# A hand-ordered retention and MLP kernel with another order of the same steps

## The chip, the cores and the metric

The kernel runs on one core of a Trainium2 chip. The metric is device time in microseconds; the median of three runs is given, and beside it one execution taken by the hardware profiler. The engines are TensorE (PE in the profile; PEld is its weight load), VectorE (DVE), ScalarE (ACT), GpSimd (POOL) and SyncE (SP), which here only issues DMAs.

## What is computed

A retention layer with 8 heads of 64, over 4 batches of 768 tokens, and behind it an MLP that mixes tokens by phase. All inputs and the output are float32.

```
state = gamma[h] * state + k[:, :, t] (outer) v[:, :, t]      # for each token t
y[:, :, t] = q[:, :, t] @ state / sqrt(64)
x = y with the heads side by side                            # [4, 768, 512]
theta = x @ w_theta
y2 = w_tok_r @ (x * cos(theta)) + w_tok_i @ (x * sin(theta)) # over tokens, each batch
u = x + y2
out = u + max(u @ w_ch, 0)
```

## The kernel before

The work is cut into small steps, each a function with a short name and a number. One string, ORDER, lists about 880 such steps by hand; the program calls them in that order, so each engine receives its instructions in the order in which the steps stand, and each DMA queue too. Engines wait for each other by semaphores. A step's last letter, where it has one, names the engine or queue that does it: v VectorE, a ScalarE, p GpSimd, s SyncE.

The retention is done in 24 units n. A unit is 256 tokens (two chunks of 128) of four heads of one batch; units 2i and 2i+1 are the two halves of the heads, and three pairs make a batch.

- Lk, Lq, Lv (line 157) load k, q and v of a unit, 256 KB each. Lth and Lch (line 174) load w_theta and w_ch, 1 MB each, into one buffer, and Lw.r.t (line 185) a block of 128 rows of a token matrix, 384 KB. All of these are issued on SP's queue.
- ck casts k to bf16 (lines 137 and 139), cq scales q by the decay (line 279), cv scales v (line 285).
- Tk and Tq transpose k and q on TensorE (line 293), four 128x128 matmuls each, and E copies the result from PSUM to kqT. Dk does all three for a unit by one DMA transpose (line 309).
- G.n is 48 matmuls of 64x64 tiles: scores A of unit n (line 323), outputs Y of unit n-1 (line 393), state products ST of unit n (line 351). m masks the scores on VectorE (line 332). SU adds up the state (lines 363 to 367), SB copies it to bf16 (two pieces a unit), and I multiplies q by the state (line 380).
- XA takes the finished x, transposed, out of PSUM on ScalarE (line 413).

The MLP is done by token blocks of 128 tokens, C for its first part and t for its second, 24 of each, six a batch.

- Tx and Ex transpose x back through PSUM (line 427), or Dx does it by DMA (line 434). Hh is theta, four matmuls of 512 columns (line 441). CN are cosine and sine on ScalarE (line 448, two a block). z multiplies them by x (line 455).
- cw casts a row block of a token matrix, Tw transposes it with six matmuls (line 472), and Ew copies it to its place in wT. cth and cch cast w_theta and w_ch in quarters.
- M.t.s is the part of token mixing for output block t that comes from input block s: two matmuls of 512 columns (line 488). It needs z of block s in the same batch and wT of row block t.
- u adds x (line 495); Tu and Eu (line 500), or Du by DMA (line 510), transpose u; O multiplies by w_ch, four matmuls (line 515); f is the last sum with the maximum (line 521); SO stores 256 KB (line 526).
- The last block, 23, is done in two halves of columns: Mh, uh, Tuh, Euh, Oh, fh, SOh (lines 529 to 576).

warm.N issues N matmuls on zeros (line 258) whose result nobody reads. const1 to const7 set up constants.

Buffers tie steps together: kf, qf and vf have nine buffers each, wtok four, wrow three, kqb five, kqT four, xT four, uT three, and all transposes through PSUM share two banks (tag "tr"). A step that writes a buffer waits until its last reader is done.

Of the kernel before, what the change touches and what calls it, by code (L numbers as in the profile page):

```python
# [32 lines left out]
I.4 CN.1.0 Tx.3 ck.6.a G.5 cq.6.v Tq.6 Lv.7.s Lk.8.s CN.1.1 Lq.8.s z.0.p SU.5 SB.5.1.p Tk.6
cw.1.0.p cv.6.p Lw.0.1.s m.5 Lv.8.s Ex.3.a XA.4.1 Hh.3 XA.4.0 ck.7.p Tx.2 cq.7.p Lk.9.s E.6.v
Lq.9.s Hh.2 Ex.2.v CN.3.0 ck.8.p SB.5.0.a z.1.v Lw.1.1.s Tw.1.0 Lv.9.s Ew.1.0.v CN.3.1 cq.8.p I.5
cv.7.p CN.2.0 z.3.v cv.8.p G.6 XA.5.1 Tk.7 XA.5.0 Hh.5 Lk.10.s Tq.7 Tk.8 CN.2.1 m.6 CN.5.1 Lq.10.s
CN.5.0 SU.6 Hh.4 E.7.v SB.6.1.a Tq.8 SB.6.0.a Tx.4 M.0.0 I.6 cw.0.1.a G.7 z.2.v E.8.v Ex.4.v Tx.5
SU.7 CN.4.1 Lw.0.2.s M.0.1 Ex.5.v ck.9.p CN.4.0 cq.9.p M.0.2 XA.6.0 Tw.0.1 SB.7.1.p XA.6.1
SB.7.0.a Lw.1.2.s m.7 z.4.v Tk.9 M.0.3 Tq.9 Ew.0.1.a cw.1.1.p I.7 Lv.10.s Lk.11.s G.8 XA.7.0
Lq.11.s z.5.v E.9.a cv.9.p Tw.1.1 M.0.4 Ew.1.1.v XA.7.1 Lw.0.3.s M.0.5 u.0 Lw.1.3.s SU.8 SB.8.0.v  # L40
Hh.6 ck.10.p cq.10.p cw.0.2.p m.8 Lw.0.4.s cw.1.2.p Tk.10 Lw.1.4.s M.1.0 Lv.11.s M.1.1 CN.6.0
cw.0.3.p M.1.2 M.1.3 Tq.10 SB.8.1.a I.8 M.1.4 Tw.0.2 M.1.5 E.10.v Lch.s cw.1.3.p Lk.12.s Lq.12.s
Ew.0.2.v Tw.1.2 CN.6.1 cv.11.p G.9 Ew.1.2.a ck.11.a Hh.7 u.1 M.2.0 ck.12.p XA.8.0 CN.7.0 CN.7.1
M.2.1 cq.11.v cq.12.p cv.10.v SU.9 Lv.12.s Lk.13.s Tk.11 XA.8.1 SB.9.1.v M.2.2 Tq.11 cv.12.p M.2.3
# [565 lines left out]
```

## Time and profile before

| | us |
|---|---|
| median of three runs | 169.86 |
| lowest and highest | 169.74, 170.08 |
| the profiled execution | 170.49 |
| its span, first to last instruction | 168.8 |
| TensorE, matmuls busy | 156.0 |
| VectorE busy | 123.8 |
| ScalarE busy | 79.2 |
| GpSimd busy | 78.5 |

HBM read is 25.69 MB and written 6.29 MB in the span. A matmul's row in the profile holds its latency (379 ns for 512 columns), though the next one starts sooner; how far apart they follow is read in the chain of waits, which lists pieces of consecutive work with their start, their length and their number. A timeline row gives start, length, engine, line, operation, the tile written and the tiles read, how many, and in brackets the idle time of the engine before it with what ended it. A row of windows gives, for a stretch of time, the busy time and number of instructions of each engine, then TensorE's granted clock as a share, the mean share of the DMA engines and GB/s. Of the slices in the page, each stands for a fortieth of the span.

### The profile page before, as it was taken

The numbers are of one execution on the slowest core, as the hardware profiler recorded it, in microseconds if no ns is written. First come the engines' busy times: TensorE is split into PE (matmuls) and PEld (weight loads), VectorE is DVE, ScalarE is ACT, GpSimd is POOL, SyncE is SP. The second block draws the span as 40 slices with busy tenths as digits, with TensorE's granted clock in tenths as the row PEclk, the third lists the DMA queues.
The fourth block names the chain that finished last, engine by engine and source line by source line (L and its number), as shares of the span: only waits on it lengthen the run. The fifth ranks groups of instructions, "written<-read, shape, count | busy, mean of one in ns | idle before, by whom it ended". The sixth has DMA issues, their size and how long they took to land.

```text
span 168.8 us, 4924 instructions
## 1 busy us (share of the span) xinstructions
PE 156.0 (92%) x2017; PEld 89.0 (53%) x2044; DVE 123.8 (73%) x200; ACT 79.2 (47%) x159; POOL 78.5 (47%) x99
## 2 busy tenths in 40 slices
PE   7988794989899989999999999999999999999991
PEld 2555463557566655555645565554555444444660
DVE  3497979699999897899669979689737443526552
ACT  6346385587657755666322593674323544000030
POOL 3778377998932634669203658023354560000000
PEclk9999999599999999999999999999999999999999
DMA  4999999999799999999999188899998736335555
GB/s 141 296 290 332 329 322 289 274 319 350 257 283 329 221 232 292 254 207 309 305 244 227 65 188 209 124 276 168 269 230 133 197 62 186 93 93 194 88 188 186
DMA packets 68582, 38.20 MB, mean 226 GB/s; under 512 B 25936, under 2 KB 63056, under 8 KB 68560
## 3 DMA queue, kind: packets, MB, share of 16 engines
q1 hardware_dynamic: 67408, 35.92, 88.8%
q10 hardware_dynamic: 1152, 1.97, 3.5%
q8 instruction: 16, 0.26, 0.6%
q14 instruction: 6, 0.05, 0.1%
HBM read 25.69 MB, written 6.29 MB: 189 GB/s over the span
## 4 chain that ended last, share of the span: by engine, by line
PE 65%; DVE 14%; SPq 11%; DMA 4%; issue 2%; ACT 1%; DVEq 0%; ACTq 0%
PE y_ps L488 31%; PE o_ps L515 11%; PE th_ps L441 9%; SPq L157 9%; DVE z L455 5%; DMA qf<-in_q_dram 4%; DVE at L332 3%; PE at_ps L323 3%; PE r_ps L393 2%; PE r_ps L380 2%; PE y_ps L538 2%; DVE kqb L279 1%; PE kq_ps L293 1%; PE w_ps L472 1%; SPq L185 1%
## 5 line engine op out<-in xcount | busy, mean ns | idle before, releaser
L488 PE MATMUL y_ps<-z,wtr 128*128 128x512 bf16 x135 | 51.2, 379 | 1.0 <-DVE z L455 0.5
L488 PE MATMUL y_ps<-z,wti 128*128 128x512 bf16 x129 | 48.9, 379 | 0.4 <-issue 0.3
L413 ACT CAST xT<-r_ps 128x256 bf16<-128x256 f32 x48 | 16.9, 372 | 30.7 <-PE r_ps L351 19.6
L279 POOL TENSOR_TENSOR kqb<-qf,qsc 128x512 bf16<-128x512 f32 x20 | 23.7, 1189 | 14.1 <-DMA qf<-in_q_dram 13.7
L332 DVE TENSOR_TENSOR at<-at_ps,mask 128x1024 bf16<-128x1024 f32 x24 | 29.1, 1213 | 1.1 <-PE at_ps L323 1.0
L521 DVE SCALAR_TENSOR_TENSOR ot<-o_ps,u 128x512 f32<-128x512 f32 x23 | 15.8, 689 | 14.9 <-PE o_ps L515 14.8
L441 PE MATMUL th_ps<-wth,xT 128*128 128x512 bf16 x89 | 25.0, 395 | 1.4 <-POOL wth L139 1.0
L285 POOL TENSOR_TENSOR vb<-vf,vsc 128x512 bf16<-128x512 f32 x17 | 18.9, 1114 | 10.0 <-DMA vf<-in_v_dram 9.9
L515 PE MATMUL o_ps<-wch,uT 128*128 128x512 bf16 x88 | 23.2, 379 | 0.4 <-DVE wch L139 0.2
L488 PEld LDWEIGHTS <-wti 128*128 128x128 bf16 x138 | 13.5, 98 | 13.4 <-issue 1.1
L448 ACT ACTIVATE cs<-th_ps,halfpi 128x512 bf16<-128x512 f32 x24 | 16.5, 688 | 8.2 <-PE th_ps L441 5.8
L488 PEld LDWEIGHTS <-wtr 128*128 128x128 bf16 x138 | 13.5, 98 | 13.0
L495 DVE TENSOR_TENSOR u<-y_ps,x_sb 128x512 bf16<-128x512 f32 x23 | 15.8, 686 | 5.8 <-PE y_ps L488 5.8
L448 ACT ACTIVATE cs<-th_ps,zerob 128x512 bf16<-128x512 f32 x24 | 16.2, 687 | 5.7 <-PE th_ps L441 5.3
L455 DVE TENSOR_TENSOR z<-cs,x_sb 128x1024 bf16<-128x1024 bf16 x18 | 16.6, 936 | 2.9 <-ACT cs L448 2.7
L455 POOL TENSOR_TENSOR z<-cs,x_sb 128x1024 bf16<-128x1024 bf16 x6 | 12.9, 2153 | 6.6 <-DMA x_sb<-xT 3.9
L139 POOL CAST kqb<-kf 128x512 bf16<-128x512 f32 x16 | 10.6, 666 | 8.3 <-DMA kf<-in_k_dram 6.1
L441 PEld LDWEIGHTS <-xT 128*128 128x128 bf16 x96 | 9.0, 100 | 10.3 <-issue 1.8
L515 PEld LDWEIGHTS <-uT 128*128 128x128 bf16 x92 | 8.7, 98 | 9.5 <-issue 0.3
L137 ACT COPY uT<-u_ps 128x512 bf16<-128x512 bf16 x6 | 3.5, 589 | 21.3 <-PE u_ps L500 21.3
L258 PE MATMUL y_ps<-zero 128*128 128x512 bf16 x36 | 12.0, 447 | 1.4 <-DVE zero L194 1.3
L293 PE MATMUL kq_ps<-ident,kqb 128*128 128x128 bf16 x112 | 9.8, 223 | 2.2 <-DVE kqb L279 2.2
(74 smaller groups left out, 209.3 us busy)
## 6 DMA issues: line engine op xcount, KB each, us to landing
kf<-in_k_dram SPq DMA_DIRECT2D x24, 256.0 KB, 5.4
qf<-in_q_dram SPq DMA_DIRECT2D x24, 256.0 KB, 5.1
vf<-in_v_dram SPq DMA_DIRECT2D x24, 256.0 KB, 5.4
out_dram<-ot SPq DMA_DIRECT2D x16, 256.0 KB, 3.3
wtok<-in_moe_w_tok_r_dram SPq DMA_DIRECT2D x6, 384.0 KB, 6.1
wtok<-in_moe_w_tok_i_dram SPq DMA_DIRECT2D x6, 384.0 KB, 5.9
out_dram<-ot ACTq DMA_DIRECT2D x7, 256.0 KB, 2.1
w<-in_moe_w_theta_dram SPq DMA_DIRECT2D x1, 1024.0 KB, 8.4
```

Of the source, the lines that this page charges most:

```text
L157: queues[e].dma_start(out=t.rearrange("p h a d -> p h (a d)"), in_=src[b, h * HU:(h + 1) * HU, i * 2 * P:(i + 1) * 2 * P, :].rearrange("h ...
L279: engines[e].tensor_mul(in_blocks(kqb_of(n)[:, 1]), by_token(raw["qf", n]), _bcast_last(K["qsc"][:, i, :, h * HU:(h + 1) * HU], D))
L285: engines[e].tensor_mul(in_blocks(vb), by_token(raw["vf", n]), _bcast_last(K["vsc"][:, i, :, h * HU:(h + 1) * HU], D))
L332: nc.vector.tensor_mul(at.rearrange("p g j a t -> p (g j) (a t)"), st["at_ps", n].rearrange("p g j a t -> p (g j) (a t)"), _bcast_mid(K["m ...
L413: nc.scalar.copy(st["xT", 2 * i + c][:, 2 * h:2 * h + 2].rearrange("p j (t a) -> p j t a", a=2), st["R", n + 1][:, c, :2 * P].rearrange("p ...
L441: nc.tensor.matmul(th_ps, st["xT", C][:, j, :], K["wth"][:, j, :], start=(j == 0), stop=(j == 3))
L448: nc.scalar.activation(st["cs", C][:, w, :], st["th_ps", C], AF.Sin, bias=K["zerob" if w else "halfpi"], scale=1.0)
L455: engines[e].tensor_mul(st["z", b][:, c], st["cs", C], _bcast_mid(x_of(C), 2))
L488: nc.tensor.matmul(st["y", t], K["wT"][r][:, s0, t0 * P:(t0 + 1) * P], st["z", b][:, s0, r, :], start=(s0 == 0 and r == 0), stop=(s0 == nT ...
L495: nc.vector.tensor_add(st["u", t], st["y", t], st["x", b][:, t0, :])
L515: nc.tensor.matmul(o_ps, st["uT", t][:, j, :], K["wch"][:, j, :], start=(j == 0), stop=(j == nD - 1))
L521: nc.vector.scalar_tensor_tensor(st["ot", t], st["o", t], 0.0, st["u", t], ALU.max, ALU.add)
```

## The change

Only the string ORDER differs; every function stays as it is. The steps stand in another order throughout, and some have another engine or another way:

| step | before | after |
|---|---|---|
| z on VectorE, GpSimd | 18, 6 | 23, 1 |
| SB on VectorE, ScalarE, GpSimd | 18, 23, 7 | 9, 31, 8 |
| cv on VectorE, GpSimd | 7, 17 | 10, 14 |
| cq on VectorE, GpSimd | 4, 20 | 6, 18 |
| ck on VectorE, ScalarE, GpSimd | 3, 5, 16 | 4, 4, 16 |
| cw on VectorE, ScalarE, GpSimd | 1, 3, 8 | 0, 5, 7 |
| cth on VectorE, ScalarE, GpSimd | 0, 2, 2 | 1, 2, 1 |
| cch on VectorE, ScalarE, GpSimd | 2, 2, 0 | 0, 0, 4 |
| Ew on VectorE, ScalarE | 8, 4 | 5, 7 |
| k and q transposed on TensorE, by DMA | 14, 10 | 12, 12 |
| E on VectorE, ScalarE | 8, 6 | 7, 5 |
| x transposed on TensorE, by DMA | 13, 11 | 15, 9 |
| Ex on VectorE, ScalarE | 8, 5 | 7, 8 |
| Eu on VectorE, ScalarE | 3, 6 | 5, 4 |
| SO on SP's queue, ScalarE's | 16, 7 | 13, 10 |
| warm-up matmuls | 40 | 43 |

The start of the two orders, down to the second M of each (what follows is changed in the same manner):

```diff
-const1 const2 const4 const3 const7 warm.8 Lk.0.s Lq.0.s ck.0.p Lv.0.s Lk.1.s const6 Lq.1.s Lv.1.s
-Lk.2.s cv.0.v Lq.2.s ck.1.a cq.0.p Tk.0 warm.4 Tq.0 E.0.v warm.4 G.0 const5 cq.1.v Lv.2.s SU.0
-SB.0.1.v Tk.1 SB.0.0.a warm.2 Tq.1 m.0 ck.2.v E.1.a Lk.3.s cv.1.p Lq.3.s warm.2 I.0 cq.2.p warm.4
-G.1 XA.0.0 Tk.2 XA.0.1 cv.2.p Lv.3.s m.1 Lk.4.s cq.3.p SU.1 ck.3.p Tq.2 E.2.a SB.1.1.a Lq.4.s
-Lth.s SB.1.0.v cv.3.p warm.7 I.1 G.2 Lv.4.s XA.1.0 Tq.3 Tk.3 XA.1.1 m.2 ck.4.a E.3.v warm.2 Tx.1
-cth.3.a SU.2 cq.4.p cth.2.p SB.2.0.v SB.2.1.v Lk.5.s warm.2 Tk.4 Tq.4 Ex.1.v Lq.5.s Lw.0.0.s
-cth.1.a warm.2 I.2 E.4.v G.3 SU.3 XA.2.1 cth.0.p SB.3.1.a Tx.0 warm.3 Hh.0 SB.3.0.v cv.4.p XA.2.0
-I.3 m.3 cq.5.v CN.0.1 ck.5.p Lv.5.s CN.0.0 cw.0.0.p Ex.0.v Lk.6.s G.4 Tk.5 SU.4 Tq.5 m.4 Lq.6.s
-Lw.1.0.s Hh.1 SB.4.0.a SB.4.1.p E.5.v XA.3.1 Tw.0.0 Lv.6.s cv.5.p Lk.7.s Lq.7.s Ew.0.0.v XA.3.0
-I.4 CN.1.0 Tx.3 ck.6.a G.5 cq.6.v Tq.6 Lv.7.s Lk.8.s CN.1.1 Lq.8.s z.0.p SU.5 SB.5.1.p Tk.6
-cw.1.0.p cv.6.p Lw.0.1.s m.5 Lv.8.s Ex.3.a XA.4.1 Hh.3 XA.4.0 ck.7.p Tx.2 cq.7.p Lk.9.s E.6.v
-Lq.9.s Hh.2 Ex.2.v CN.3.0 ck.8.p SB.5.0.a z.1.v Lw.1.1.s Tw.1.0 Lv.9.s Ew.1.0.v CN.3.1 cq.8.p I.5
-cv.7.p CN.2.0 z.3.v cv.8.p G.6 XA.5.1 Tk.7 XA.5.0 Hh.5 Lk.10.s Tq.7 Tk.8 CN.2.1 m.6 CN.5.1 Lq.10.s
-CN.5.0 SU.6 Hh.4 E.7.v SB.6.1.a Tq.8 SB.6.0.a Tx.4 M.0.0 I.6 cw.0.1.a G.7 z.2.v E.8.v Ex.4.v Tx.5
-SU.7 CN.4.1 Lw.0.2.s M.0.1 Ex.5.v ck.9.p CN.4.0 cq.9.p M.0.2 XA.6.0 Tw.0.1 SB.7.1.p XA.6.1
...
+const1 const2 const4 const3 const7 warm.8 Lk.0.s ck.0.v Lq.0.s Lv.0.s Lk.1.s Tk.0 cq.0.v const5
+cv.0.v warm.2 Tq.0 const6 E.0.v Lq.1.s Lv.1.s ck.1.p Lk.2.s warm.10 G.0 Lq.2.s cq.1.v Tk.1 Lv.2.s
+cv.1.v Tq.1 Lw.0.0.s Lk.3.s Lq.3.s m.0 SU.0 Lv.3.s ck.2.p Lk.4.s E.1.v cq.2.p Lq.4.s warm.3 Tk.2
+SB.0.1.p SB.0.0.a cq.3.p Lth.s Lv.4.s warm.3 Tq.2 Lk.5.s cv.3.p E.2.a warm.1 I.0 cw.0.0.a G.1
+cv.2.v cth.0.p SU.1 SB.1.1.v ck.3.a m.1 XA.0.1 SB.1.0.a warm.3 Tw.0.0 XA.0.0 warm.3 Tq.3 Lq.5.s
+Tk.3 ck.4.v I.1 Ew.0.0.a G.2 SU.2 Lv.5.s cv.4.p E.3.a XA.1.1 SB.2.0.a m.2 SB.2.1.a XA.1.0 cq.4.v
+cth.3.a cth.2.a warm.10 I.2 G.3 Lk.6.s Lq.6.s Tq.4 cth.1.v ck.5.p XA.2.0 SU.3 XA.2.1 SB.3.0.a
+Lw.1.0.s Tk.4 Hh.1 cq.5.p Lw.0.1.s cv.5.p Hh.0 E.4.v Lv.6.s SB.3.1.v Tx.0 ck.6.p I.3 m.3 G.4
+Ex.0.v Tk.5 m.4 CN.1.0 Tq.5 CN.1.1 cq.6.p CN.0.1 SU.4 Tx.1 Lk.7.s Lw.1.1.s cv.6.p E.5.v XA.3.0
+Lq.7.s CN.0.0 SB.4.1.v Lw.0.2.s SB.4.0.v Hh.2 Tk.6 Ex.1.a XA.3.1 Tq.6 Lv.7.s z.1.v Tx.2 I.4 ck.7.p
+z.0.v G.5 SU.5 E.6.v Lk.8.s cw.0.1.a CN.2.1 SB.5.0.p Hh.3 SB.5.1.v cq.7.p m.5 Tw.0.1 Lq.8.s
+cw.0.2.p cw.1.0.a Lv.8.s Ex.2.v XA.4.1 XA.4.0 I.5 G.6 Ew.0.1.v cv.7.p SU.6 Tk.7 CN.3.0 cw.1.1.a
+cq.8.p Tq.7 ck.8.p CN.2.0 CN.3.1 E.7.v XA.5.1 Tx.3 Lk.9.s Tw.1.0 Lw.1.2.s Hh.5 Ex.3.v cv.8.p
+SB.6.1.a z.2.v XA.5.0 m.6 SB.6.0.a z.3.v Ew.1.0.a Tx.5 Lq.9.s I.6 Ex.5.a CN.5.0 Hh.4 CN.5.1 Tw.0.2
+Tq.8 G.7 Tk.8 Ew.0.2.v SU.7 CN.4.1 M.0.0 XA.6.0 Lw.0.3.s cw.1.2.p Tx.4 E.8.v M.0.1 Ex.4.a Lv.9.s
...
```

The stretch of the new order in which w_ch is cast and the first unit, 11, goes through a DMA transpose:

```diff
+M.1.0 M.1.1 SU.8 M.1.2 SB.8.1.a Lch.s m.8 Lq.11.s
+cv.9.v M.1.3 SB.8.0.p E.9.a Lv.11.s M.1.4 Tw.1.3 cch.1.p XA.7.1 M.1.5 I.8 Tx.7 cv.10.v G.9 cch.2.p
+ck.10.a u.1 Ex.7.a XA.8.0 M.2.0 ck.11.p Ew.1.3.v Tk.10 Tq.10 Tx.6 E.10.a SU.9 m.9 cch.0.p M.2.1
+Lw.0.4.s cw.0.4.p Lw.1.4.s M.2.2 SB.9.1.a M.2.3 SB.9.0.a M.2.4 XA.8.1 M.2.5 cq.11.v cw.1.4.p
+Lk.12.s ck.12.p Ex.6.v Tu.0 I.9 Lq.12.s Lw.0.5.s Dk.11 Eu.0.v CN.6.1 u.2 cch.3.p G.10 Lw.1.5.s
+cq.12.p Lv.12.s z.6.p cw.1.5.p Tu.1 XA.9.1 Lk.13.s Lq.13.s SU.10 ck.13.p cq.13.p Dk.12 Eu.1.v Hh.7
```

The two ends:

```diff
-Mh.0.0 u.20 Mh.0.1 Mh.1.0 Mh.0.2 Mh.0.3 SO.18.a Mh.0.4 Mh.0.5 uh.0 O.19 Tu.20 Mh.1.1 SO.22.s f.19
-Mh.1.2 Eu.20.a Mh.1.3 Mh.1.4 Mh.1.5 uh.1 SO.17.s Tuh.0 O.20 Euh.0 f.20 Tuh.1 O.21 SO.19.s Euh.1
-Oh.0 Oh.1 f.21 SO.20.a SO.21.a fh.0 SOh.0 fh.1 SOh.1
+M.21.2 M.21.3 Tu.19 Eu.19.v O.17 f.17 M.21.4 M.21.5 u.21 SO.13.a O.19 Mh.0.0 Mh.1.0 Mh.0.1 Mh.0.2
+Mh.0.3 Mh.0.4 Mh.0.5 SO.22.a Mh.1.1 Mh.1.2 Mh.1.3 Tu.21 Du.20 Mh.1.4 f.19 Mh.1.5 uh.0 SO.17.a
+Eu.21.a Tuh.0 uh.1 O.20 Tuh.1 Euh.0 O.21 SO.19.a Euh.1 f.20 SO.20.a Oh.0 Oh.1 f.21 fh.0 fh.1
+SO.21.s SOh.0 SOh.1
```

## The prediction

> **What bounds the kernel now.** I read the page's busy shares and slices first, then the chain of waits in order of time, then the windows around the one dip of the clock, and last the timeline there.
>
> ```profile
> PE 156.0 (92%) x2017; PEld 89.0 (53%) x2044; DVE 123.8 (73%) x200; ACT 79.2 (47%) x159; POOL 78.5 (47%) x99
> ...
> PE   7988794989899989999999999999999999999991
> ...
> PEclk9999999599999999999999999999999999999999
> ```
>
> TensorE is full from about slice 11 on; its only gaps, and the one slice at half clock, lie in the first 40 us. The chain gives prices of matmuls that follow each other:
>
> ```profile
> 119.37 0.22 PE r_ps L380 x4
> 119.60 0.35 PE at_ps L323 x16
> ...
> 139.10 3.88 PE y_ps L488 x18
> 142.98 0.86 PE o_ps L515 x4
> ```
>
> So a 512-column matmul costs 3.88/18 = 0.216, four 128-column ones 0.22, six (Tw) 0.34. A whole G costs about 0.91: 0.35 for A, 0.35 for Y, 0.22 for ST by their mean pitch and the bubble behind them. With these I keep a ledger: **lost time** of a step is its start less all real matmul work ordered before it (warm-ups are no work). Before M.0.0 stand 18 Tk/Tq (4.0), G.0 to G.6 (0.57 + 6 x 0.91), I.0 to I.5 (1.1), six Hh (5.2), five Tx (1.1), two Tw (0.67): 18.1 us. The trace has M.0.0 at 37.97: lost 19.9. The whole program is 145.3 us of work and its last matmul ends at about 164.9: lost 19.6. The kernel loses everything before 38 us and nothing after, so the time is work + lost start + the 3.9 us of last store behind the last matmul.
>
> Where the start is lost:
>
> ```profile
> 26.05 2.12 POOL L455 TENSOR_TENSOR z<-cs,x_sb 128x1024 bf16<-128x1024 bf16 x1
> ...
> 26.32 2.40 DVE L279 TENSOR_TENSOR kqb<-qf,qsc 128x512 bf16<-128x512 f32 x1 [0.39 <-DMA qf<-in_q_dram]
> ...
> 28.78 0.62 PE L293 MATMUL kq_ps<-ident,kqb 128*128 128x128 bf16 x8 [2.18 <-DVE kqb L279]
> ```
> ```profile
> core 0: us, PE busy (x) PEld busy (x) DVE busy (x) ACT busy (x) POOL busy (x), PEclk, DMA share, GB/s
> 22.93:26.35 3.42, 3.24 (x88) 2.18 (x82) 3.04 (x7) 2.98 (x7) 2.53 (x4) 1.00 1.14 321
> 26.35:29.76 3.41, 1.18 (x38) 0.89 (x28) 3.41 (x3) 1.43 (x4) 2.46 (x3) 1.00 1.12 283
> 29.76:33.18 3.42, 3.42 (x16) 1.82 (x16) 2.24 (x4) 1.94 (x4) 3.42 (x4) 0.50 0.98 276
> ...
> 19.52:22.93 3.41, 2.39 (x59) 1.36 (x57) 2.21 (x5) 2.90 (x7) 2.85 (x4) 1.00 1.14 326
> ```
>
> VectorE's scaling of q 6 took 2.40 where its other rows take 0.68 to 0.8: it got through only when GpSimd's z, 2.12 long, had ended at 28.17. TensorE idled 2.18 for it (lost time 15.35 at G.5, 17.38 at Tq.6), was busy 1.18 of those 3.41 us, and then had half its clock for 3.41 us (17.39 at Hh.3, 19.06 at I.5). A window with 2.39 busy (19.52 to 22.93) was followed by no dip.
>
> **The change part by part.**
>
> Work of TensorE: Tk and Tq go from 14 to 12 each (two more kqT by DMA transpose), Tx from 11 + 2 to 15 (two fewer x by DMA). That is -4 x 0.22 + 2 x 0.22 = -0.44 us. Warm-ups go from 40 to 43 matmuls; they cost only where real work is ready: the ten before I.2 (10 x 0.216 = 2.2) start behind G.2 near 16.9 and end at 19.1, while SB.2, which I.2 needs, is done near 18.2: 0.9 that the wait for theta below swallows.
>
> Work moved between engines, whole program, mean of each row: GpSimd loses five z (-10.6), three cv, two cq, and gains four wch casts: about -15. VectorE gains five z (4.7), three cv, two cq, a ck, a wth cast and two Eu, loses nine SB (-4.3), three Ew and two wch casts: about +3. ScalarE gains eight SB, three Ew, three Ex, two cw and loses E, Eu and wch casts: about +5, with three more stores issued on its queue (0.35 each). DMA transposes stay 35 (issue 1.2 to 1.4 each on SP), bytes stay. Dk.11 is new on SP's queue and waits there for cq.11 near 52 us; behind it stand the loads from w row 1.5 and unit 12 on. Dk.12 landed 5.2 after its issue here; with that v 12 is there by 60, and G.12, with 47.7 in front, comes at 66: cost 0, with 6 us of cover. All that lies after 38 us is hidden under TensorE's full stretch, whose engines are at 73% and 47%; if one of these falls late there, its wait adds to the end one for one.
>
> The start, step by step. G.0: VectorE now does ck.0, cq.0, cv.0 and only then four memsets of 0.27 and E.0 (0.68). Its v lands at 6.0, so 6.1 + 0.7 + 1.1 + 0.7 = 8.5 against 7.51: 1.0 later. That need not stay, since loads set the pace next.
>
> Theta weights: one more 384 KB row block is loaded ahead of w_theta. Row blocks took about 1.1 each here, so theta lands at 19.75 + 1.1 = 20.85, casts 0.6 to 0.7 each follow, Hh.1 starts near 21.6 with 6.3 of work in front: lost 15.3 (before 14.7 at Hh.0).
>
> q 6: the same 6.68 MB stand ahead of it in both orders, so it lands at 26.30 again. Now GpSimd scales it (row 1.04) and z.0 is VectorE's: Tq.6 at 27.4 with 11.1 in front: lost 16.3 against 17.4. The idle time in that stretch falls to about 1 us of 3.4, close to the window that kept its clock, so I let the half clock (1.7 us) go.
>
> q 8 is late next. Three more row blocks are loaded before it. In front of it and with it are 26 blocks of 256 KB, five of 384 KB and theta, 9.83 MB; here that sum is reached with q 9, which the trace has landing at 35.75. GpSimd's cq.8 1.04, then Tq.8 at 36.9, with 18.44 of work in front: lost **18.5**. If bytes flowed at the 313 GB/s of the page's slice there (350 at best), it would be 18.0 to 19.1. The other chains that I followed through the rows end just below: ScalarE, back to back from w row 0.1 (28.5) through cw (moved there from GpSimd, and now waiting for that load with CN.2, XA.4 and CN.3 queued behind it), XA, CN, Ew to Ex.5, lets Tq.8 go at 36.5 (18.1); VectorE, from cth.1 at 21.5 through E.7 near 33.5, lets Tw.1.0 go with 15.7 in front (17.8). With three chains this close and hops of 0.05 to 0.1 between engines, I take 18.8, nearer to the load's bound than to the 19.9 of now, at M.0.0, 38.6 us with 19.8 in front (the 18.1 from above, G.7, I.6 and two Tw).
>
> After that I see no load near its due time, and the end has the same shape: Oh, f.21, fh, two half stores. One store moves from ScalarE's queue to SP's, 0.33 of issue that ends before fh.0 does; cost 0.
>
> Sum: profiled span 168.8 - 0.44 - (19.87 - 18.8) = 167.3. The profiled run itself took 170.49 with that span, 0.63 over the median of 169.86; I apply the difference, -1.5, to the median: **168.4**.
>
> The Trainium skill, "TensorE: Matmul & The Clock Gate", sections "Why this matters for your kernels" and "Part 4: PE-mode transpose", asks for no idle gaps over about 3 us to keep the clock, and says that transposes do not count as busy in the same way. Here 2.18 us within one stretch were enough, so the measurement decides against the first. The second speaks against this change: by it the stretches around Tq.4 to Hh.1 and Tq.6 would look emptier than I count, the dip would come again, and the sum would be up to 170.1.
>
> **The rivals.**
>
> *The clock dips again.* For it: TensorE still waits about 1 us in several stretches between 20 and 37 us, and no row lies between 1.18 and 2.39 busy. Against: none of these waits is 2 us. Price 1.7 where work is waiting, 0 where the load of q 8 comes later anyway: up to 168.4 + 1.7 = 170.1, I take 169.8.
>
> *VectorE sets the start* (the one on the slower side). Between G.0 and z.5 it has 6 E (4.1), 3 Ew (1.65), 3 Ex (1.2), 5 SB (2.6), 14 pieces of SU (4.1), 8 masks (9.7), 6 z (5.6), 3 cq, 2 cv, a ck, a cth (4.6): 33.5 us at mean rows, 33.0 before. Before, z.5 ended at 43.67, 36.2 after G.0: 3.2 of idling. With the same idling z.5 ends at 8.5 + 33.5 + 3.2 = 45.2, M.0.5 with 24.4 in front has lost 20.8, and the time is 169.86 - 0.44 + 0.9 = 170.3; with one more wait behind GpSimd as that of q 6 (1.7) 172. I take 171. It decides once VectorE idles over 1.2 in that stretch beyond what I assume (z.5 after 43.2). Against: z no longer runs 2.12 long on GpSimd, and GpSimd's work plus VectorE's from SBUF falls from 33.7 to 31.7 there.
>
> *The gain is given back later*: a transposed uT or x lands late, or w_ch, whose casts GpSimd must all do now and which are queued before ck.11, waits for its load. O.0 has 37.6 in front, 56 us; the casts should be done at 54. The margin of 2 us is thin: 169.2 to 170.5.
>
> **How the numbers follow.** Forecast 0.62 (own range 167.4 to 169.3), clock 0.12, VectorE 0.16, given back 0.10. A run of this kernel tells 0.2% (0.34 us) from no change. Faster: 0.62 and about a third of clock's and given back's 0.22, 0.70; same 0.10; slower 0.20. The range 167.3 to 170.3 leaves out most of VectorE's case and a start below the load's pace.
>
> **What would show it.** Right: no stretch of half clock between 6 us and the end; Tq.6 near 27.4, Tq.8 near 36.9 behind a q that landed at 35.7; M.0.0 near 38.6; no lost time after. Wrong: a slice of PEclk at 5; z.5 after 43.2; a row of idle before TensorE past 45 us that names a DMA transpose, wch or z.

## The result, and the profile after

| | before | after |
|---|---|---|
| median, us | 169.80 (4 executions, 169.53 to 170.08) | 169.64 (169.43, 169.53, 169.75 and one of 179.84) |
| ratio | | 0.9986, 95% interval 0.9962 to 1.001 |
| the profiled execution, us | 170.49 | 169.43 |
| its span | 168.8 | 167.6 |

No difference that this measurement can tell, where 168.4 was forecast. The ratios here and below leave out executions that lie more than 1.5% above the fastest of their kernel; an execution like the 179.84 therefore shows in counts and not in ratios, and the experiments have a part of their own on it.

The page of the changed kernel, busy shares and slices, shows no slice with half the clock:

```profile
PE 153.9 (92%) x2011; PEld 87.4 (52%) x2039; DVE 117.7 (70%) x197; ACT 83.3 (50%) x169; POOL 61.8 (37%) x92
...
PE   7878976789999979999999999999999999999991
...
PEclk9999999999999999999999999999999999999999
```

VectorE (117.7 against 123.8) and GpSimd (61.8 against 78.5) have less to do. TensorE has a thin slice in the start, as before, and a new one, the 15th, near 60 us.

The timeline of the changed kernel in its start (the columns are start, length, engine, line, operation, tiles, number, and in brackets the idle time ahead of it with what ended it):

```profile
26.00 1.04 POOL L279 TENSOR_TENSOR kqb<-qf,qsc 128x512 bf16<-128x512 f32 x1
26.92 0.69 ACT L448 ACTIVATE cs<-th_ps,halfpi 128x512 bf16<-128x512 f32 x1
27.67 1.02 PE L441 MATMUL th_ps<-wth,xT 128*128 128x512 bf16 x3 [1.39 <-ACT cs L448]
28.53 0.61 PE L293 MATMUL kq_ps<-ident,kqb 128*128 128x128 bf16 x8
...
34.99 0.50 PE L472 MATMUL w_ps<-ident,wrow 128*128 128x128 bf16 x6 [0.56 <-DVE kqT L139]
...
36.31 1.05 POOL L279 TENSOR_TENSOR kqb<-qf,qsc 128x512 bf16<-128x512 f32 x1 [0.62 <-DMA qf<-in_q_dram]
...
37.72 0.39 PE L293 MATMUL kq_ps<-ident,kqb 128*128 128x128 bf16 x4
...
38.97 0.38 PE L488 MATMUL y_ps<-z,wtr 128*128 128x512 bf16 x1
```

cq.6 ends on GpSimd at 27.04, as foreseen, but TensorE isn't there: Hh.2 stands ahead of Tk.6 and Tq.6 and waits 1.39 us for a PSUM bank which the cosine CN.0.0 (the row at 26.92) frees. Tq.6 starts at 28.75, lost 17.62 by the ledger of the prediction. Tw.1.0 then waits 0.56 for E.7 on VectorE and has lost 19.28. From there to Tq.8, at 37.72, TensorE loses nothing more (19.29): q 8 had landed at 36.15 and was scaled at 37.36, in time for its turn. M.0.0 starts at 38.97: lost 19.17.

The same view 20 us later:

```profile
55.89 1.59 DVE L285 TENSOR_TENSOR vb<-vf,vsc 128x512 bf16<-128x512 f32 x1
...
56.89 2.57 POOL L455 TENSOR_TENSOR z<-cs,x_sb 128x1024 bf16<-128x1024 bf16 x1
57.51 2.10 DVE L139 CAST sbd<-s 64x256 bf16<-64x256 f32 x1
...
59.65 0.69 DVE L521 SCALAR_TENSOR_TENSOR ot<-o_ps,u 128x512 f32<-128x512 f32 x1
...
60.39 1.02 PE L515 MATMUL o_ps<-wch,uT 128*128 128x512 bf16 x4 [1.10 <-DVE ot L521]
```

z.6, the one z left on GpSimd, runs 2.57 us, and SB.10.1 on VectorE, which takes 0.3 elsewhere (31.26 to 31.58 for SB.5.1), stands 2.10 behind it. f.0 is queued behind SB.10.1 on VectorE, O.1 needs the bank that f.0 reads: TensorE idles 1.10. Not every execution has this wait: in profiles of kernels below that keep z.6 and SB.10.1 in their places it is 1.46 (after_cch_undone), 0.77 (after_warm) and 0.63 (after_cn_loads), and there is none in after_again and after_sb51, which come to this place 2 us later. Lost 20.11 at Tu.2, and 18.89 at the last matmuls. Between them TensorE gains on the ledger, whose prices for small matmuls are a little high: where nothing waits behind M.0.0, it drifts down by 0.7 (best4 below) to 1.5 (after_z6v).

### The profile page after: what moved, and what is told of

The parts are those of the page before. It is cut to its first block, busy times and chain, and to the rows that moved or that the text cites. A ratio compares the mean times of both kernels' runs of the same rounds, so it can differ in the third digit from the quotient of the medians.

```text
span 167.6 us, 4915 instructions
## 1 busy us (share of the span) xinstructions
PE 153.9 (92%) x2011; PEld 87.4 (52%) x2039; DVE 117.7 (70%) x197; ACT 83.3 (50%) x169; POOL 61.8 (37%) x92
## 2 busy tenths in 40 slices
DMA packets 69606, 38.46 MB, mean 230 GB/s; under 512 B 26960, under 2 KB 64080, under 8 KB 69584
## 4 chain that ended last, share of the span: by engine, by line
PE 75%; DVE 8%; SPq 7%; DMA 5%; issue 2%; ACT 2%; DVEq 0%
PE y_ps L488 34%; PE o_ps L515 11%; PE th_ps L441 10%; SPq L157 6%; DMA w<-in_moe_w_theta_dram 5%; PE at_ps L323 4%; PE r_ps L393 3%; DVE at L332 2%; PE r_ps L380 2%; PE kq_ps L293 2%; PE x_ps L427 2%; PE w_ps L472 2%; DVE sbd L139 2%; PE y_ps L538 2%; PE r_ps L351 2%
## 5 line engine op out<-in xcount | busy, mean ns | idle before, releaser
L279 POOL TENSOR_TENSOR kqb<-qf,qsc 128x512 bf16<-128x512 f32 x18 | 19.3, 1070 | 19.6 <-DMA qf<-in_q_dram 17.1
L441 PE MATMUL th_ps<-wth,xT 128*128 128x512 bf16 x89 | 23.8, 379 | 2.0 <-ACT cs L448 1.4
L448 ACT ACTIVATE cs<-th_ps,zerob 128x512 bf16<-128x512 f32 x24 | 16.3, 688 | 9.0 <-PE th_ps L441 5.7
L455 DVE TENSOR_TENSOR z<-cs,x_sb 128x1024 bf16<-128x1024 bf16 x23 | 17.1, 759 | 3.1 <-ACT cs L448 2.8
L137 ACT CAST sbd<-s 64x256 bf16<-64x256 f32 (+1 forms) x31 | 11.3, 365 | 12.5 <-DVE s L363 6.5
L285 POOL TENSOR_TENSOR vb<-vf,vsc 128x512 bf16<-128x512 f32 x14 | 15.2, 1092 | 6.2 <-DMA vf<-in_v_dram 4.3
L137 ACT COPY uT<-u_ps 128x512 bf16<-128x512 bf16 x4 | 2.4, 588 | 21.6 <-PE u_ps L500 21.6
L323 PE MATMUL at_ps<-kqT 64*64 64x128 bf16 x384 | 10.0, 222 | 1.9 <-DVE at L332 1.4
```

The lines of the kernel that those rows point to most:

```text
L279: engines[e].tensor_mul(in_blocks(kqb_of(n)[:, 1]), by_token(raw["qf", n]), _bcast_last(K["qsc"][:, i, :, h * HU:(h + 1) * HU], D))
L285: engines[e].tensor_mul(in_blocks(vb), by_token(raw["vf", n]), _bcast_last(K["vsc"][:, i, :, h * HU:(h + 1) * HU], D))
L323: nc.tensor.matmul(at_ps[cols, g, j, a, :], kqT[rows, 0, a, j, cols], kqT[rows, 1, :, j, cols], start=(j == 0 and a == 0), stop=(j == 1 an ...
L441: nc.tensor.matmul(th_ps, st["xT", C][:, j, :], K["wth"][:, j, :], start=(j == 0), stop=(j == 3))
L448: nc.scalar.activation(st["cs", C][:, w, :], st["th_ps", C], AF.Sin, bias=K["zerob" if w else "halfpi"], scale=1.0)
L455: engines[e].tensor_mul(st["z", b][:, c], st["cs", C], _bcast_mid(x_of(C), 2))
```

## The experiments

### What half of before's executions pay

Before unchanged, profiled once more:

> The kernel before, unchanged, to see what its ordinary executions look like. Theory A (the stretch of half clock from 29.8 to 33.2 us in the profile of before is an accident of that execution, which took 170.49 us where the median is 169.8): clocks near 1.0 and spans near 168.0 in most runs, a new profile without the stretch or with it elsewhere, lost time at M.0.0 near 19.2 in place of 19.9. Theory B (the stretch belongs to the kernel, and the changed order gave its gain back by other means that its profile does not show): every run has a clock of 0.99 and the new profile has the stretch again, lost time 19.9.

169.92 median against 170.5 of before run beside it (ratio 0.9999, 0.9947 to 1.0051). Four of the 12 executions have a clock of 0.99 or less, so neither theory holds for all of them. The profiled one kept its clock. Its windows and its timeline:

```profile
core 0: us, PE busy (x) PEld busy (x) DVE busy (x) ACT busy (x) POOL busy (x), PEclk, DMA share, GB/s
...
26.32:29.73 3.41, 1.38 (x17) 0.93 (x15) 3.24 (x4) 1.62 (x4) 2.47 (x3) 1.00 1.08 280
29.73:33.15 3.42, 3.37 (x74) 2.27 (x73) 3.42 (x6) 3.17 (x7) 3.42 (x4) 1.00 0.98 307
```
```profile
28.33 0.62 PE L293 MATMUL kq_ps<-ident,kqb 128*128 128x128 bf16 x8 [1.98 <-DVE kqb L279]
...
35.56 0.38 PE L488 MATMUL y_ps<-z,wtr 128*128 128x512 bf16 x1
```
```profile
123.39 1.36 SPq L309 DMA_TRANSPOSE kqT<-kqb  x1
...
128.72 0.42 PE L323 MATMUL at_ps<-kqT 64*64 64x128 bf16 x16 [1.21 <-DMA kqT<-kqb]
```

The same wait of 1.98 us for cq.6, but no half clock behind it, and M.0.0 comes at 35.56 instead of 37.97: lost 17.46 instead of 19.87. Of this 1.21 is given back at G.23, which then comes before its DMA transpose has landed (issued 123.39); the last matmuls have lost 18.94, and the span is 168.2.

Over all jobs (a job is a set of kernels measured together on one chip) 175 executions of before carry a clock: 81 lie at 0.991 or less, median 171.22, and 94 above, median 169.17. So about half the executions have a stretch of half clock, and those are about 2 us longer.

A direct test: eight warm-up matmuls ahead of Tq.6, where TensorE waits.

```diff
-G.5 cq.6.v Tq.6 Lv.7.s Lk.8.s CN.1.1 Lq.8.s
+G.5 cq.6.v CN.1.1 warm.8 Tq.6 Lv.7.s Lk.8.s Lq.8.s
```

> The kernel before with eight more warm-up matmuls (1.7 us of TensorE on zeros) where TensorE waits 2 us for cq.6; the wait itself, the loads and all work stay. Theory that the half clock, not the wait, is what half of the executions of before pay: TensorE idles under 0.6 us there, no execution at a clock of 0.991 or less, all near those of before at full clock (168.5 to 170), median 1 to 2 us under a median of before that holds both kinds; M.0.0 lost 17.3 to 17.8. Rival, that the executions at 0.99 are slow for another reason, loads for one: as many of them as in before, at 171.

None of 12 executions at 0.991 or less (all 0.996 or more), where 13 of 29 of before beside it were; highest 170.32 where before went to 172.0. So the long executions of before go with the half clock: matmuls without a use, which by themselves can only delay, take both away. The median, 169.34, is 0.4 under before's 169.73 and not 1 to 2, and the ratio shows no gain (1.0023, 0.9993 to 1.0054). The profile shows one reason:

```profile
26.80 2.67 POOL L455 TENSOR_TENSOR z<-cs,x_sb 128x1024 bf16<-128x1024 bf16 x1
26.81 0.68 DVE L279 TENSOR_TENSOR kqb<-qf,qsc 128x512 bf16<-128x512 f32 x1
...
27.49 1.89 PE L258 MATMUL y_ps<-zero 128*128 128x512 bf16 x7
...
29.22 0.61 PE L293 MATMUL kq_ps<-ident,kqb 128*128 128x128 bf16 x8
```

In this execution cq.6 got in ahead of z.0 and was done at 27.49. There was no wait to fill, and the warm-ups stood in front of work that was ready: M.0.0 has lost 18.38, not 17.3 to 17.8.

### z.0 on VectorE, alone

```diff
-Lq.8.s z.0.p SU.5 SB.5.1.p Tk.6
+Lq.8.s z.0.v SU.5 SB.5.1.p Tk.6
```

> The kernel before with z.0 alone moved from GpSimd to VectorE. Theory that the wait of cq.6 behind GpSimd's z.0 costs the start what the profile shows: cq.6 takes 0.7 to 1.0 in place of 2.40, TensorE's 2.18 us gap falls under 0.8, no half clock, 0.7 to 1.5 us faster (168.3 to 169.1). Rival, that the loads and VectorE's other work set the start anyway: the gap goes, but M.0.0 comes no earlier than 37.5, and the time stays within 0.3 us of 169.8.

168.45 against 170.5, ratio 0.991 (0.9865 to 0.9954). With z.0 off GpSimd, VectorE's scaling of q 6 has its short time (first row), the wait of TensorE falls from 2.18 to 0.49, and M.0.0 comes at 34.92, lost 16.82. The timeline of this kernel:

```profile
26.31 0.69 DVE L279 TENSOR_TENSOR kqb<-qf,qsc 128x512 bf16<-128x512 f32 x1 [0.41 <-DMA qf<-in_q_dram]
26.92 0.69 DVE L455 TENSOR_TENSOR z<-cs,x_sb 128x1024 bf16<-128x1024 bf16 x1
...
27.05 0.62 PE L293 MATMUL kq_ps<-ident,kqb 128*128 128x128 bf16 x8 [0.49 <-DVE kqb L279]
```

The same kernel in a later job:

> The kernel before with z.0 on VectorE once more, beside the others of this job. Expected as it was: 168.0 to 168.8 median, at most one execution in ten at a clock of 0.99, 0.5 to 1.3 per cent under the fast runs of before.

169.05 against 169.73, ratio 0.9964 (0.9918 to 1.001); one execution of 12 at a clock of 0.99, as in the first. By the ratio the gain lies between 0.4% and 0.9% on these two, the second within its interval of nothing. Between executions above 0.991 alone the medians are 168.40 against 169.46 of before in the first job, and 169.03 against 168.85 in the second. So it is shown that this kernel seldom has the half clock (two of 24 executions); that it gains anything beyond that isn't shown.

Then the wait that gives it back at G.23. k 23 and q 23 are loaded right behind q 22, and Dk.23 stands right behind cq.23:

```diff
-Lk.22.s Lq.22.s cq.22.p
+Lk.22.s Lq.22.s Lk.23.s Lq.23.s cq.22.p
...
-cq.23.p M.14.5 I.20 f.10
+cq.23.p Dk.23 M.14.5 I.20 f.10
```

> The kernel before with the loads of k and q 23 and the DMA transpose of unit 23 moved forward in SP's queue (Lk.23, Lq.23 behind Lq.22, Dk.23 ahead of Dx.18). Theory that an execution of before at full clock starts 2.4 us earlier than the profiled one, and gives 1.2 of that back at G.23, which waits for Dk.23: gap before G.23 gone, executions at full clock 0.9 to 1.3 us faster (near 168.3), executions at a clock of 0.99 unchanged (171.3). Rival, that something else is late next to it: under 0.4 us.

A miss: 171.34, ratio 1.0123 (1.0067 to 1.0178), and 9 of 12 executions had the low clock; the three others have a median of 169.85, where 168.3 was expected. In the profile the wait at G.23 is gone, but G.21 waits 0.79 for its own transpose at 118.34 and two M wait 0.54 and 0.57 for z at 140.8 and 142.8: something that the two earlier loads set back on SP's queue, it seems; what, wasn't followed. Both edits together:

> The kernel before with both edits: z.0 on VectorE, and unit 23's loads and transpose moved forward. Theory: lost time at M.0.0 16.5 to 17.2, no stall after it, clock 1.0 in nearly all, time 167.0 to 167.5, 2 us or more under both kernels. Rival: the gain of one edit is taken by the next late thing, 168.0 to 168.5.

168.56 against 170.09, where 167.0 to 167.5 was expected; no low clock, and a ratio of 1.0002 (0.996 to 1.0044). No better than z.0 alone.

### The two waits of the changed kernel

z.6 goes to VectorE behind f.1; or SB.10.1 to ScalarE:

```diff
-cq.12.p Lv.12.s z.6.p cw.1.5.p
+cq.12.p Lv.12.s cw.1.5.p
...
-Tw.0.5 f.1 M.4.0
+Tw.0.5 f.1 z.6.v M.4.0
```
```diff
-Lv.14.s SB.10.1.v SB.10.0.a Tx.9
+Lv.14.s SB.10.1.a SB.10.0.a Tx.9
```

> The changed kernel with its last GpSimd z, z.6, moved to VectorE behind f.1, where VectorE idles 0.88 us. Theory that the 1.25 us which TensorE loses at 59 to 60 us come from SB.10.1 (2.10 us) waiting for this z on the shared port, with f.0 and O.1 behind it: SB.10.1 0.2 to 0.5, no gap before O.1, span 166.4 to 166.6, time 168.3 to 168.6. Rival, that VectorE is simply late there: a gap of over 0.6 stays before O.1 and the time is within 0.4 us of 169.6.

The wait ahead of O.1 is gone; span 166.0, the last matmuls have lost 17.3 (after: 18.9). 168.84 median (168.3 to 168.6 expected), ratio 0.9984 (0.994 to 1.0028), three of 12 at 183 to 186.

> The changed kernel with SB.10.1 on ScalarE, z.6 left on GpSimd. Same theory from the other side: nothing of VectorE that reads SBUF stands between z.6 and f.0, so f.0 starts when O.0 is done near 57.5, no gap before O.1, 0.9 to 1.25 us faster than the changed kernel (168.3 to 168.8). Rival (VectorE late, or ScalarE then late with xT): time within 0.4 us of 169.6.

The wait is gone here too (span 167.4, M.0.0 19.64, end 18.65), and 170.28 is the median (168.3 to 168.8 expected) because five of 12 took 179 to 181; ratio 0.9975 (0.9918 to 1.0032). So where O.1 waits it is for GpSimd's z.6, by way of SB.10.1 and f.0: taking away either ends the wait. In the ledger that is worth about 1 us; the times don't show it, since both intervals hold 1.

For the start, CN.0.0 ahead of XA.3.0 on ScalarE, and two of the row blocks of w that stand ahead of q 8 (1.1 and 0.2) behind it, with their casts (and Tw.0.2 and E.8 in turn):

```diff
-CN.0.1 SU.4 Tx.1 Lk.7.s Lw.1.1.s cv.6.p E.5.v XA.3.0
-Lq.7.s CN.0.0 SB.4.1.v Lw.0.2.s SB.4.0.v Hh.2
+CN.0.1 CN.0.0 SU.4 Tx.1 Lk.7.s cv.6.p E.5.v XA.3.0
+Lq.7.s SB.4.1.v SB.4.0.v Hh.2
...
-Tw.0.1 Lq.8.s
+Tw.0.1 Lq.8.s Lw.1.1.s Lw.0.2.s
```

> The changed kernel with two edits to its start: CN.0.0, which frees the bank that Hh.2 waits 1.39 us for, ahead of XA.3.0; and two of the row blocks (w rows 1.1 and 0.2) loaded behind q 8, with their casts and the transpose Tw.0.2 behind the work on unit 8. Theory that bank and loads together set the start: no gap over 0.5 before Hh.2, q 8 lands near 34, M.0.0 lost 17.6 to 18.4 (19.2 in the changed kernel), 0.7 to 1.3 us faster than it. Rival, that VectorE's run of work sets it: M.0.0 lost 18.8 or more, within 0.3 us of the changed kernel.

Hh.2 waits 0.37 instead of 1.39, q 8 lands at 33.92 instead of 36.15, yet M.0.0 comes at 38.34, lost 18.54: only 0.6 of 2.2 us is won, since I.5 waits 0.75 for SB.5.0 on GpSimd and Tw.1.0 still 0.56 for E.7 on VectorE. Neither theory's number. 168.65, ratio 0.9971 (0.9931 to 1.0012), one of 12 above 175.

### Executions of 175 to 186 us

The changed kernel again:

> The changed kernel, unchanged, beside the kernel before on the same chip. Theory that the change took the start out of reach of the half clock but starts later than an execution of before at full clock: its times spread less over 168.9 to 170, clock 1.0 in nearly all that are not far off, equal to before's executions at full clock within 0.4 us and about 1.8 us under those at 0.99; M.0.0 lost 18.8 to 19.7, gap before O.1 of 1 us. Rival, that the change is a plain gain of 1 us: its executions are 1 us under before's full-clock ones.

Three of six above 175, so the theory of a smaller spread fell; of 175 executions of before none is above 175 (highest 173.57). A first thought was that the w_ch casts, all on GpSimd now and read late, held O.0. They went back to ScalarE and VectorE:

```diff
-cch.1.p
...
-cch.2.p
...
-cch.0.p
...
-cch.3.p
+CN.6.1 cch.1.a cch.0.a u.2 cch.2.v G.10
...
+Eu.1.v cch.3.v Hh.7
```

> The changed kernel with the four w_ch casts back on ScalarE and VectorE, two each, as the kernel before has them. Theory that VectorE is locked out of the port it shares with GpSimd for as long as GpSimd has a next instruction ready, and that the w_ch casts make that run long when the loads are ahead: no execution over 173 in 12 (4 of 10 in the changed kernel), the others within 0.6 us of the changed kernel's 169.4 to 169.8. Rival, that the long executions come from the loads or the DMA transposes: 3 to 6 of 12 over 175.

Five of 12 above 175: this theory fell (169.65; ratio 1.0026, 0.9985 to 1.0067).

The next kernel has after_cn_loads' edits, z.6 on VectorE behind f.1, and cw.1.2 behind SB.7.1:

> The changed kernel with the two edits to its start (CN.0.0 early; two row blocks, their casts and Tw.0.2 behind unit 8), z.6 on VectorE behind f.1, and cw.1.2 behind SB.7.1 on GpSimd, which I.7 waited 0.57 us for. Theory that each removes a wait that TensorE has no other work for: no gap over 0.5 after M.0.0, M.0.5 lost 18.3 to 18.8, span 165.8 to 166.4, time 167.5 to 168.2. Rival, that the loads' own jitter between executions is as large as what is left: 168.3 to 169.

168.83, ratio 0.9972 (0.9934 to 1.0011): the rival's number. Its profile happens to be of a long execution, 179.15. Its timeline:

```profile
50.70 1.17 POOL L135 CAST wch<-w 128x512 bf16<-128x512 f32 x2
51.67 6.12 DVE L281 TENSOR_TENSOR vb<-vf,vsc 128x512 bf16<-128x512 f32 x2
51.82 0.61 POOL L135 CAST kqb<-kf 128x512 bf16<-128x512 f32 x1
...
52.93 1.59 POOL L135 CAST wrow<-wtok 128x768 bf16<-128x768 f32 x2
...
55.61 1.04 POOL L275 TENSOR_TENSOR kqb<-qf,qsc 128x512 bf16<-128x512 f32 x1
57.25 0.32 PE L347 MATMUL r_ps<-vb,kqb 64*64 64x64 bf16 x16 [2.99 <-DVE vb L281]
```

cv.9 and cv.10, two instructions of about 0.7, took 6.12 us on VectorE while GpSimd ran a row of nine without a gap, from 50.70 to 56.64, the last eight of them beside cv.9. cq.11 stands behind them on VectorE, Dk.11 on SP's queue waits 11.5 us for cq.11, and the loads stand behind Dk.11; the page shows the hole, in the 13th and 14th slice, 53 to 62 us:

```profile
GB/s 149 284 321 326 309 296 310 342 339 326 352 339 32 0 218 279 226 285 189 309 319 60 183 306 208 77 190 277 187 226 124 209 108 191 78 168 61 233 65 177
```

So cv.9, cv.10 and cq.11 go to GpSimd itself, with cch.3 next to cch.0; on top of best2, and then on top of the changed kernel with z.6 moved:

```diff
-cv.9.v M.1.3 SB.8.0.p
+M.1.3 SB.8.0.p cv.9.p
...
-Tx.7 cv.10.v G.9
+Tx.7 G.9
...
-Lw.0.4.s cw.0.4.p
+Lw.0.4.s cq.11.p cw.0.4.p
...
-m.9 cch.0.p M.2.1
+m.9 cch.0.p cch.3.p M.2.1
```

> best2 with VectorE's three instructions on SBUF that fall into GpSimd's run (cv.9, cv.10, cq.11) put on GpSimd itself, cv.9 and cv.10 ahead of the w_ch casts where GpSimd waits for w_ch, and cch.3 next to the other casts. Same theory: no execution over 173, since nothing of VectorE waits for the port there; median 167.6 to 168.6, under best2's 168.83. Rival, that GpSimd, now longer by 3 us there, makes w_ch or the row blocks late: a gap over 0.6 before O.0 or Tw.1.4, median 168.8 or more.

168.73 against 169.74, ratio 0.9937 (0.9901 to 0.9972). The highest of 11 is 173.29, so both numbers of the theory were just missed; the gap of the rival is not in the profile. The second of the two:

> Kernel after with cv.9, cv.10 and cq.11 on GpSimd, cch.3 next to cch.0, and z.6 on VectorE behind f.1. Theory (VectorE's casts cv.9 and cv.10 are kept out by GpSimd's unbroken row of instructions, cq.11 behind them holds Dk.11 and the loads behind it): no execution above 175 us, the others 168 to 169. Rival (the long executions come from elsewhere, the start or the chip): 3 to 6 of 12 above 175, as in after.

The theory is not enough: still three of 13 above 175, and the profile is of one of them, 178.72. The hole in the middle is gone, and the whole loss is in the start. Its timeline:

```profile
34.06 0.39 POOL L139 CAST sbd<-s 64x256 bf16<-64x256 f32 x1 [2.32 <-DVE s L365]
34.42 1.03 POOL L279 TENSOR_TENSOR kqb<-qf,qsc 128x512 bf16<-128x512 f32 x1
34.56 5.37 DVE L139 CAST sbd<-s 64x256 bf16<-64x256 f32 x1
...
35.41 0.82 POOL L139 CAST wrow<-wtok 128x768 bf16<-128x768 f32 x1
36.19 1.04 POOL L285 TENSOR_TENSOR vb<-vf,vsc 128x512 bf16<-128x512 f32 x1
...
38.74 1.03 POOL L285 TENSOR_TENSOR vb<-vf,vsc 128x512 bf16<-128x512 f32 x1
...
40.03 0.59 PE L380 MATMUL r_ps<-kqT,sbd 128*128 128x128 bf16 x4 [4.86 <-POOL vb L285]
```

SB.5.1, the cast that takes 0.32 in the changed kernel's own profile, takes 5.37: it begins 0.5 behind GpSimd's SB.5.0, six more instructions follow there without a gap, and it ends 0.16 after the last of them (39.77). I.5 on TensorE waits 4.86. The releaser that the row names, GpSimd's vb, is not what I.5 reads; it is where the row ended that kept VectorE out. Whether the row has a gap goes with the loads: in the profile of the changed kernel GpSimd waited 0.81 for q 7 at that place, here Tq.6 was already 2.9 us later (lost 20.49 against 17.62), and GpSimd waited for no load. The empty stretch then costs the clock, in windows of the same kernel:

```profile
35.92:39.34 3.42, 0.00 (x0) 0.00 (x0) 3.42 (x1) 1.32 (x3) 3.42 (x5) 1.00 1.07 330
39.34:42.75 3.41, 2.10 (x56) 1.92 (x57) 2.79 (x5) 0.00 (x0) 0.44 (x1) 0.50 1.11 335
42.75:46.16 3.41, 2.83 (x20) 2.06 (x20) 3.04 (x6) 2.13 (x5) 0.61 (x1) 0.50 1.15 324
```

Is the clock what starts it? Five warm-ups (the expectation says eight) ahead of Hh.2, in the changed kernel:

> Kernel after with eight warm-up matmuls in the 1.39 us wait ahead of Hh.2. Theory (the half clock at the start of some executions is what makes them long later): no execution above 175 us, the median 169 to 169.6. Rival (the start has no part in it): 3 to 6 of 12 above 175.

Two of 12 above 175: neither theory's number, so filling that wait doesn't end them, and whether it makes them rarer isn't shown (168.82, ratio 0.998, 0.9938 to 1.0022). The other way: take away the wait of SB.5.1 by giving it to ScalarE, as one word in three kernels.

```diff
-SB.5.0.p Hh.3 SB.5.1.v cq.7.p
+SB.5.0.p Hh.3 SB.5.1.a cq.7.p
```

> Kernel best3 with SB.5.1 on ScalarE. Theory (SB.5.1 on VectorE waits 2.05 us behind GpSimd's row ck.7, SB.5.0, cq.7, cv.7, and the late I.5 leaves TensorE idle long enough for the half clock): median 168.0, none above 170.5. Rival (ScalarE takes its order's next steps as late): 168.7 and some of 172 to 173, as best3.

> Kernel after with one word changed: SB.5.1 on ScalarE. Theory (the long executions are those in which SB.5.1 on VectorE stands 2 to 5.4 us behind GpSimd's unbroken row, as in the profile of after_unlock): none of the executions above 175 us, the median 168.3 to 169.3. Rival (cv.9 and cv.10 at 51 us are kept out too and make long ones by themselves): still 2 to 5 of 12 above 175.

> Kernel after_unlock with SB.5.1 on ScalarE, so that neither place is left. Theory: none above 172 us, the median 168 to 168.8 (the wait ahead of O.1 is gone too). Rival (a third cause): still some above 175.

Medians 168.07, 169.56 and 168.26; ratios 0.9938 (0.9884 to 0.9993), 0.9961 (0.9922 to 1.0) and 0.99 (0.9867 to 0.9934). No execution of the three is above 175 (highest 171.76, 174.06 and 173.25). The upper bounds of best4 (170.5) and after_unlock_sb51 (172) were each missed by one execution, and after_sb51 missed its median of 168.3 to 169.3. best4 and after_unlock_sb51 have the lowest medians of the study, 168.07 against 170.28 and 168.26 against 170.19 of before beside them.

| SB.5.1 stands on | executions | above 175 us |
|---|---|---|
| VectorE: the changed kernel, and with z.6, SB.10.1, w_ch, cv and cq or warm-up edits | 71 | 22 |
| VectorE, with the w loads moved behind q 8 (after_cn_loads, best2, best3) | 35 | 2 |
| ScalarE (best4, after_sb51, after_unlock_sb51) | 35 | 0 |
| GpSimd: before | 175 | 0 |

In pairs that differ in SB.5.1 alone it is 4 of 10 against none of 12 for the changed kernel, 3 of 13 against none of 11 for after_unlock, and none of 11 against none of 12 for best3, which has none anyway. after_sb51 and after_unlock_sb51 ran on a chip on which the changed kernel did not, so by the counts alone a difference between chips is not ruled out, though every job that had changed kernels with SB.5.1 on VectorE had long executions of them. The traces settle more.

The profile of after_unlock_sb51 is of its longest execution, and as late as that of after_unlock up to Tq.6 (lost 20.22). Its timeline at the same place:

```profile
34.42 0.40 ACT L137 CAST sbd<-s 64x256 bf16<-64x256 f32 x1 [2.56 <-DVE s L365]
34.52 0.40 POOL L139 CAST sbd<-s 64x256 bf16<-64x256 f32 x1 [2.65 <-DVE s L365]
34.88 1.04 POOL L279 TENSOR_TENSOR kqb<-qf,qsc 128x512 bf16<-128x512 f32 x1
...
36.27 0.38 PE L380 MATMUL r_ps<-kqT,sbd 128*128 128x128 bf16 x4 [0.65 <-ACT xT L413]
```

The same cast beside the same row on GpSimd takes 0.40 on ScalarE, I.5 waits 0.65 instead of 4.86, and the span is 171.6 instead of 177.0. So the two traces show what the wait of SB.5.1 costs an execution that starts late, and the counts make it the main cause of those above 175; those of 181 to 186 were never profiled. That cv.9 and cv.10 can be kept out in the same way is shown once, in best2. What makes the start 2 to 3 us later in some executions wasn't followed to its end. In after_unlock's profile Hh.1 waits 1.31 for the theta weights' cast on GpSimd (1.27 in after_sb51's), I.3 waits 0.90 for SB.3.1, and a first stretch of half clock lies from 29.09 to 32.51, ahead of SB.5.1.

## Why the forecast failed, by its own steps

**The failed step is the sum**, "profiled span 168.8 - 0.44 - (19.87 - 18.8) = 167.3", and the difference of -1.5 applied to the median. The term 19.87 is a lost start with the half clock in it. That stretch was seen and told, but the sum takes it as part of every execution, without a reason; it comes in 81 of 175. At full clock the start of before loses 17.46, so the changed start, 19.17, is 1.7 later and not 1.1 earlier. By the profile of before at full clock the end loses 18.94, and the changed kernel's 18.89: with the -0.44 of work the sum is 168.2 - 0.44 - 0.05 = 167.7, and 167.6 was measured. 0.6 is gained between two executions at full clock, not 1.5. Against the profile on which the sum was built the span did fall by 1.2 (168.8 to 167.6), not far from the forecast; the error was to carry that over to a median which stands for other executions too. The median moved by 0.16. "0.2% (0.34 us)" as what a run tells was taken from three executions in the same way: the 175 lie between 167.07 and 173.57.

**Work of TensorE**, -0.44: right by the count (144.87 against 145.31 in the ledger).

**Work of the others**: GpSimd -16.7 against -15 and ScalarE +4.1 against +5, but VectorE -6.1 against +3. The mean rows of before had waits behind GpSimd in them: z took 0.94 on VectorE there and 0.76 after, cq 1.15 and 0.73. The bytes that the DMAs move went from 38.20 to 38.46 MB.

**G.0, theta**: 8.38 against 8.5; Hh.1 lost 15.11 against 15.3. Right.

**q 6**: "Tq.6 at 27.4", lost 16.3. cq.6 was done at 27.04, but Tq.6 came at 28.75 with 17.62. The wait of Hh.2 for CN.0.0's bank, 1.39 us, was overlooked: a step ahead of the followed one in TensorE's queue, with a reader on a third engine.

**q 8**: landing 36.15 against 35.75, Tq.8 37.72 against 36.9. The load's bound was 0.4 short. But it isn't what bound: the chain of VectorE through E.7 put 17.8 on Tw.1.0, 19.28 came, and Tq.8 (19.29) found its q ready. Making q 8 land 2.2 earlier (after_cn_loads) moved M.0.0 by only 0.6, and there too Tq.8 has lost what Tw.1.0 has (18.66 and 18.65).

**M.0.0**: lost 19.17 against 18.8, at 38.97 against 38.6. The size is 0.4 off, and that it is no more is partly luck: the pace was set by VectorE's chain, 1.5 later than told, and not by the load. So the VectorE rival was right about the engine in the start, though not about its price (it has 20.8 lost at M.0.5, where 19.07 was measured).

**No half clock**: right in this profile (its emptiest window, 24.72 to 28.13, has 1.95 us busy). In the profiled long executions it came.

**No lost time after 38 us**: wrong by 1.10 ahead of O.1. That before loses nothing there was a misreading too: its profile has waits of 0.48, 0.18 and 0.23 between 43 and 62 us, which the ledger's drift hides. The VectorE rival names this mechanism, a wait behind GpSimd, but in the start, with z.5 as its mark; z.5 ended at 43.06, below its mark of 43.2. The third rival, gain given back later, names another place. The rows that carried it, GpSimd's z 2.12 long and VectorE's cast of 0.3 behind it, were those of cq.6 over again, at z.6.

**w_ch**: casts to be done at 54; the last ended at 55.93, and O.0 started at 56.41. The margin was thinner than told, and cost nothing in this profile.

## What to carry to other kernels

Before a term is taken from one profiled execution, ask which of its waits would not come again: a stretch of half clock behind a wait of 2 us came in half the executions here, and a change that removes it gains only there. Where VectorE stands behind GpSimd, the price of an instruction is not its own length. Mostly it was one instruction of the other engine, and in a few places the whole row that GpSimd ran without a gap; a forecast should hold both prices, the more so as that row was closed in an execution that came late and open in one that did not. The small cast on the path was better off on ScalarE, where it took 0.40 beside the same row: one word, SB.5.1 on ScalarE, went with the end of executions 10 us too long. z.0 off GpSimd alone gave before 0.9% in one job and 0.4% in another, the second within its interval of nothing, and between executions at full clock only in the first.

## What the hardware showed that I had not expected

- VectorE isn't always let in between GpSimd's instructions: 5.37 us for a cast of 0.32 beside a row of seven (after_unlock), 6.12 us for two of 0.7 beside a row of nine (best2). I had counted on one instruction's length (2.12, as for cq.6), and that is the common case. Ten us earlier in after_unlock the same kind of cast, SB.3.1, got in at the first end of an instruction, though GpSimd went on without a gap:

```profile
24.10 1.04 POOL L279 TENSOR_TENSOR kqb<-qf,qsc 128x512 bf16<-128x512 f32 x1
...
24.15 1.14 DVE L139 CAST sbd<-s 64x256 bf16<-64x256 f32 x1
...
25.10 1.09 POOL L285 TENSOR_TENSOR vb<-vf,vsc 128x512 bf16<-128x512 f32 x1
```

  In the 20 profiles, 206 of VectorE's instructions from SBUF to SBUF were under way when GpSimd passed from one instruction to the next without a gap. 194 were done within 0.61 us of that moment; 12 stayed out until the row ended, at four places (SB.5.1, cv.9, cv.18 and one z). What decides between the two, no run here shows.
- TensorE's busy share of a window doesn't by itself tell whether the clock falls. The stretches between two changes of the granted clock in these profiles are multiples of 3.41 us (3.41, 6.83 and 23.89 in after_unlock), so the windows are laid from such a change. In windows of 3.41 us, 1.18 busy (38 matmuls, before) and 1.68 busy (63 matmuls, after_unlock, 25.68 to 29.09) were followed by half clock, while 1.38 busy (17 matmuls, before_again) was not. The Trainium skill, "TensorE: Matmul & The Clock Gate", section "Part 4: PE-mode transpose", says that transposes do not count as busy in the same way; that would fit the first two, but no run here separates transposes from the other small matmuls.
- One DMA transpose that waited in SP's queue stopped all loads behind it: 0 GB/s in a slice of 4.4 us (best2), with 11.5 us of waiting for cq.11.
